# Top-32 attention and a gated feed-forward on one core: one operand of the pairwise minimum and maximum, and of the weights' bit operations, read from PSUM, under a planner with other durations

## The chip, the core and the metric

The kernel runs on one core of a Trainium2 chip. A core has TensorE (PE, matrix products), VectorE (DVE), ScalarE (ACT), GpSimd (POOL) and SyncE (SP, which here issues all DMAs). Each engine works through its own queue in order; a semaphore holds an instruction until what it needs is done. SBUF is the working memory, PSUM the eight banks that PE writes into. POOL does not read PSUM in this kernel. The metric is device microseconds of one execution; smaller is better.

## The reference, cut to what matters

```python
# q, k, v: (4 batches, 8 heads, 576, 64) float32
scores = scale * np.matmul(q, k.transpose(0, 1, 3, 2))
kth = np.partition(scores, -32, axis=-1)[..., -32:-31]
scores = np.where(scores >= kth, scores, -1e9)
attn = exp(scores - max); attn = attn / (sum + 1e-9)
x = matmul(attn, v)                       # heads side by side: (2304, 512)
xn = x / sqrt(mean(x * x) + 1e-6) * rms_g
g = xn @ w_gate                           # (2304, 1536)
out = (g * sigmoid(g) * (xn @ w_val)) @ w_out
```

The three weights arrive as float64 and are used as float32 in two parts, a rounded one and the remainder, so that products keep float32 accuracy.

## The kernel before, in words

**Plan.** `build` does not issue instructions; it adds operations to a `_Plan`, each with its engine, a duration, the tiles it reads and writes, at times a PSUM bank, and a priority `pri`. `emit` then runs a greedy list schedule (`place`): at each time every free engine takes the ready operation with the smallest key. Forward and backward passes alternate, each using the other's times as keys, and the order of the shortest plan found is what every engine's queue gets, DMA issues on SP included. The durations steer only this order; the hardware takes its own time. Banks fall into three groups: "a" (four banks: scores, transposes, value products, preparation of Q and K), "g" (two: gate and value products) and "o" (two: output products). A bank is chosen when the first operation on it is placed and is free after the last.

**Attention.** There are 72 steps; each handles two score tiles `e` of 128 queries by 576 keys. In `attend`, PE makes the scores of a tile in two halves of 288 columns, each in an "a" bank, and ScalarE copies each half into an SBUF tile `sp` (L523). `topk` then finds the 32nd largest of a row on VectorE: the pairwise minimum and maximum of the two halves (L497, L498), the 8 largest of the minima (L499), then four rounds of "8 largest" (L502) and three of "replace those 8" (L504). `bt` (L530) gathers the row's maximum and threshold times constants. ScalarE's Relu against the threshold (L534), GpSimd's subtraction (L535) and ScalarE's Exp (L536) make the masked weights; PE transposes them (L560), ScalarE copies (L562), and PE multiplies with V. The scores have four `sp` buffers, so PE may run ahead of VectorE.

The two lines that the change is about:

```python
add(DVE, 0.37, lambda: nc.vector.tensor_tensor(mn[:, e, :], a, b, op=ALU.min), r=spk, w=(nk,), pri=pri)
add(DVE, 0.37, lambda: nc.vector.tensor_tensor(row[:, 0:half], a, b, op=ALU.max), r=spk, w=(mk,), pri=pri)
```

**Feed-forward.** Each unit (256 tokens, early on 128) normalises its rows (small VectorE chains, L539 to L541 and L639 to L645; L628 scales rows out of a bank), transposes them, forms the two parts (ScalarE L658, VectorE L661), and makes gate and value products in "g" banks. Tanh, two products (L710 and L711, or GpSimd's L707 and L708 in place of L710), and a split into two parts (L722, L723) lead to the output products. All matmuls are recorded at L298, the helper that issues them.

**Weights.** During the first unit, `weight_piece` loads 36 pieces of 128 x 512 float64 as 32-bit words and rebuilds a float32 in a tile `t` with VectorE's bit operations: for the gate weights three instructions (L337 to L339), for the other two matrices two (L332, L333) with a correction by ScalarE and GpSimd (L334, L335). Each later one reads `t` as the one before wrote it. ScalarE and GpSimd then split `t` (L340, L343).

A second plan, `build(True)`, with thresholds from whole rows, is run only if a flag says that the shortcut of the pairs missed something; no instruction of it is in the profile.

Of the kernel before, what the change touches and what calls it, by code (L numbers as in the profile page):

```python
# [22 lines left out]
# Where an op's first key lies against its step's, and which forms some of the ops take.  # L23
# [14 lines left out]
class _Bank:  # L38
    """One PSUM bank's worth of data; the bank itself is chosen when the first op is placed."""
# [11 lines left out]
class _Plan:  # L51
    """Ops are added in an order in which they would be right one after another; emit() puts them
    out in the order of a greedy list schedule that keeps every dependency of that order."""
# [8 lines left out]
    def add(self, eng, dur, fn, r=(), w=(), bank=None, pri=0.0, nbytes=0):  # L62
        o = _Op()
        o.eng, o.dur, o.fn, o.pri, o.bank, o.nbytes = eng, dur, fn, pri, bank, nbytes
# [29 lines left out]
    def place(self, key, back=False):  # L94
        """A greedy list schedule, the op with the smallest key first; back: from the end. Returns its
        length and every op's start, or None if it gets stuck on the banks."""
# [5 lines left out]
        free = [0.0] * 4 + [0.0 if back else 0.45]  # L102
        avail = [0.0] * len(ops)
# [9 lines left out]
        while left:  # L113
            for e in range(5):
# [74 lines left out]
    def emit(self):  # L189
        """Schedules forwards and backwards by turns, each with the other's times as keys."""  # L190
# [19 lines left out]
def tile_topk_attention_moe(  # L210
# [80 lines left out]
    def build(exact):  # L291
        """The whole computation as a plan; exact: with the threshold from whole rows, and with the
        weights as they were left by the other one."""
# [20 lines left out]
        def weight_piece(src, half, hi, lo, keyh, keyl, pri):  # L314
            """[128, 512] of a weight as hi + lo. A float64 comes as its bits."""
# [8 lines left out]
            else:  # L324
# [4 lines left out]
                dma(raw, src.bitcast(U32), 524288, (), rk, pri - 2)  # L329
                if half:  # L330
                    ti, si = t.bitcast(I32), lo.bitcast(I32)
                    add(DVE, 0.336, lambda: nc.vector.tensor_scalar(tu, low, 29, None, op0=ALU.logical_shift_right), r=rk, w=tk, pri=pri)  # L332
                    add(DVE, 0.602, lambda: nc.vector.scalar_tensor_tensor(tu, top, 3, tu, op0=ALU.logical_shift_left, op1=ALU.bitwise_or), r=rk, w=tk, pri=pri)  # L333
                    add(ACT, 0.62, lambda: nc.scalar.activation(lo, top.bitcast(F32), AF.Sign), r=rk, w=(keyl,), pri=pri)  # L334
                    add(POOL, 1.23, lambda: nc.gpsimd.tensor_tensor(ti, ti, si, op=ALU.add), r=(keyl,), w=tk, pri=pri)  # L335
                else:
                    add(DVE, 0.336, lambda: nc.vector.tensor_scalar(tu, top, 3, 0x3FFFFFF8, op0=ALU.logical_shift_left, op1=ALU.bitwise_and), r=rk, w=tk, pri=pri)  # L337
                    add(DVE, 0.602, lambda: nc.vector.scalar_tensor_tensor(tu, top, 0xC0000000, tu, op0=ALU.bitwise_and, op1=ALU.bitwise_or), r=rk, w=tk, pri=pri)
                    add(DVE, 0.602, lambda: nc.vector.scalar_tensor_tensor(tu, low, 29, tu, op0=ALU.logical_shift_right, op1=ALU.bitwise_or), r=rk, w=tk, pri=pri)  # L339
            add(ACT, 0.52, lambda: nc.scalar.copy(hi, t), r=tk, w=(keyh,), pri=pri)  # L340
            add(
                POOL, 1.225,
# [4 lines left out]
        def weight_in(c, n, pri):  # L347
            """The nth of the 8 pieces of gate's and val's columns c * 512 and on."""
# [12 lines left out]
        ptc = [0, 0]  # L361

        def split(bank, hi, lo, keyh, keyl, pri):
# [5 lines left out]
            add(POOL, 1.225, lambda: nc.gpsimd.tensor_tensor(lo, tmp, hi.bitcast(F32), op=ALU.subtract), r=(keyh, tk), w=(keyl,), pri=pri)  # L369
# [64 lines left out]
        def prep_q_tile(b, tile, half, pri):  # L434
            """128 queries of four heads."""
# [35 lines left out]
        # A row of mx: the larger ones of the pairs (288), the 8 largest of the smaller ones, then the  # L471
        # rounds of eight, so that the last of those 8, the row's maximum and its 32nd are 15 apart.
# [5 lines left out]
        def topk(i, e, pri):  # L478
            """The 32 largest of a row: pairs' larger ones and the 8 largest of their smaller ones hold
            them unless a ninth smaller one is above the 32nd, which attend() notes down."""  # L480
# [15 lines left out]
            a, b = sp[s][:, e * S:e * S + half], sp[s][:, e * S + half:(e + 1) * S]  # L496
            add(DVE, 0.37, lambda: nc.vector.tensor_tensor(mn[:, e, :], a, b, op=ALU.min), r=spk, w=(nk,), pri=pri)  # L497
            add(DVE, 0.37, lambda: nc.vector.tensor_tensor(row[:, 0:half], a, b, op=ALU.max), r=spk, w=(mk,), pri=pri)  # L498
            add(DVE, 0.37, lambda: nc.vector.max(row[:, half:half + 8], mn[:, e, :]), r=(nk,), w=(mk,), pri=pri)  # L499
            for n in range(4):  # L500
                o8 = row[:, rounds[n]]
                add(DVE, 0.376, lambda o8=o8: nc.vector.max(o8, row[:, 0:half + 8]), w=(mk,), pri=pri + 0.1 * n)  # L502
                if n < 3:
                    add(DVE, 0.376, lambda o8=o8: nc.vector.match_replace(row[:, 0:half + 8], o8, row[:, 0:half + 8], NEG), w=(mk,), pri=pri + 0.1 * n)  # L504

        def attend(i, scores, qs, sums, pri):
            """scores(e): the (column in qh/ql, K slot) pairs that add up to tile e's scores."""
            s, t = i % NS, i % 2
            for e in range(2):
                for half in range(2):  # L510
# [11 lines left out]
                    add(PE, 0.252 * len(parts), sm, r=(("qh", qs), ("ql", qs)) + kk, w=(("sp", s, e, half),), bank=bank, pri=pri + PR["SO"])  # L522
                    add(ACT, 0.29, lambda bank=bank, c0=c0: nc.scalar.copy(sp[s][:, c0:c0 + 288], bank.tile[:, 0:288]), w=(("sp", s, e, half),), bank=bank, pri=pri + PR["SO"])  # L523
            for e in range(2):
                topk(i, e, pri + PR["TB"] * e)
# [3 lines left out]
            else:  # L529
                add(DVE, 0.075, lambda: nc.vector.tensor_tensor(bt[t], mx[:, :, 295:326:15], cst, op=ALU.mult), r=(("mx", 0, 0), ("mx", 1, 0)), w=(("bt", t),), pri=pri + PR["SM"])  # L530
                add(POOL, 0.154, lambda: nc.gpsimd.tensor_tensor(gap[:, i, :], bt[t][:, :, 0], bt[t][:, :, 2], op=ALU.subtract), r=(("bt", t),), w=(("gap", i),), pri=pri + PR["SM"])
            for e in range(2):
# [3 lines left out]
                add(ACT, 0.76, lambda e=e, tl=tl: nc.scalar.activation(tl, tl, AF.Exp, bias=bt[t][:, e, 1:2], scale=SCALE, accum_out=sums(e)[0]), r=(("bt", t),), w=spkeys(i, e) + (sums(e)[1],), pri=pri + PR["SM"])  # L536

        def invert(rslot, sl, keys, key, pri):
            add(DVE, 0.08, lambda: nc.vector.tensor_scalar(rs[rslot][sl], rs[rslot][sl], 1e-9, None, op0=ALU.add), w=keys, pri=pri)  # L539
            add(DVE, 0.09, lambda: nc.vector.reciprocal(ri[rslot][sl], rs[rslot][sl]), r=keys, w=(key,), pri=pri)  # L540
# [25 lines left out]
        def attend_out(i, j, pair, vs, pri):  # L566
# [9 lines left out]
            add(PE, 1.26, pv, r=(ck, ak, bk) + vkeys(vs), w=(("xv", j, pair),), bank=bank, pri=pri)  # L576
# [31 lines left out]
        wcount = [0, 0]  # L608

        def feed_forward(u, js, xs, xkeys, rslot, stores, pri, last=False):  # L610
            """For the tiles js of 128 tokens: both, or one."""
# [27 lines left out]
            add(DVE, 0.07, lambda: nc.vector.tensor_scalar(s_, s_, 1.0 / DM, 1e-6, op0=ALU.mult, op1=ALU.add), w=ssk, pri=fx)  # L639
            add(DVE, 0.07, lambda: nc.vector.tensor_scalar(w_.bitcast(I32), s_.bitcast(I32), 1, None, op0=ALU.logical_shift_right), r=ssk, w=rwk, pri=fx)  # L640
            add(DVE, 0.07, lambda: nc.vector.tensor_scalar(v_.bitcast(I32), w_.bitcast(I32), -1.0, float(0x5F3759DF), op0=ALU.mult, op1=ALU.add), r=rwk, w=rvk, pri=fx)
            for _ in range(3):
                add(DVE, 0.07, lambda: nc.vector.scalar_tensor_tensor(w_, v_, -0.5, v_, op0=ALU.mult, op1=ALU.mult), r=rvk, w=rwk, pri=fx)  # L643
                add(DVE, 0.07, lambda: nc.vector.tensor_tensor(w_, w_, s_, op=ALU.mult), r=ssk, w=rwk, pri=fx)
                add(DVE, 0.07, lambda: nc.vector.scalar_tensor_tensor(v_, w_, 1.5, v_, op0=ALU.add, op1=ALU.mult), r=rwk, w=rvk, pri=fx)  # L645
# [230 lines left out]
```

## Time and profile before

| | |
|---|---|
| median of 3 runs | 956.7 us (955.13 to 957.41) |
| span of the profiled execution | 955.8 us |
| mean granted TensorE clock | 0.946 |
| PE busy | 842.4 us (88%) |
| DVE busy | 834.2 us (87%) |
| ACT busy | 655.1 us (69%) |
| POOL busy | 540.2 us (57%) |

The profiled execution has no time of its own beside its span; the span lies between the three runs. A row of a stretch reads "from:to length, then for each engine busy us (instructions), the granted TensorE clock, the DMA share and GB/s"; for one source line it holds VectorE's busy time and count alone, then the same three. A row of one source line reads "engine, operation, out<-in, count: shortest/median/longest ns, first and last start". A row of a group reads "busy us, mean ns | idle time of the engine before it". A row of the timeline reads "start us, duration us, engine, line, operation". A row of waits reads "who <- for whom: us in total, times, longest". A recorded duration overlaps the next instruction's by about 0.08 us, so that differences of durations are used and not their sums.

### The profile page before, as it was taken

How to read it: one execution, taken by the hardware profiler on the slowest of the kernel's cores; microseconds unless marked ns; L12 is line 12 of the kernel's file. 1: busy time of each engine (PE TensorE's matmuls, PEld its weight loads, DVE VectorE, ACT ScalarE, POOL GpSimd, SP SyncE). 2: the span in 40 equal slices, each digit the busy share in tenths (PEclk: the TensorE clock that was granted, in tenths of full speed). 3: DMA queues.
4: the chain of work that ended last, by engine and by line, in shares of the span. 5: the costliest groups of instructions: out<-in, count | busy, mean ns of one | idle time of the engine just before them, and what ended most of it. 6: DMA issues, size and time to landing. Idle time of an engine off the chain costs nothing. (4 is left out here: it accounts for less than half of the span.)

```text
span 955.8 us, 19213 instructions
## 1 busy us (share of the span) xinstructions
PE 842.4 (88%) x6458; PEld 756.4 (79%) x6458; DVE 834.2 (87%) x2472; ACT 655.1 (69%) x1655; POOL 540.2 (57%) x564
## 2 busy tenths in 40 slices
PE   6655664778989999999999999998999999999996
PEld 4544554567778988998799889898999899899995
DVE  6999999999899999999889999999999929895221
ACT  6856565658878887887778788786877736765311
POOL 6756787696666754677656555565535423532111
PEclk9966786889999999999999999999999999999999
DMA  6432564345554333332443243343533433333433
GB/s 170 124 118 71 175 192 150 126 155 183 179 155 124 107 87 125 102 93 79 141 124 116 68 140 96 94 114 101 162 103 102 128 114 103 112 91 108 134 118 107
DMA packets 104573, 116.84 MB, mean 122 GB/s; under 512 B 68880, under 2 KB 82192, under 8 KB 104464
## 3 DMA queue, kind: packets, MB, share of 16 engines
q1 hardware_dynamic: 104464, 115.51, 39.7%
q8 instruction: 53, 0.87, 0.4%
q14 instruction: 56, 0.46, 0.2%
HBM read 104.47 MB, written 11.01 MB: 121 GB/s over the span
## 5 line engine op out<-in xcount | busy, mean ns | idle before, releaser
L502 DVE MAX8 mx<-mx 128x8 f32<-128x296 f32 x576 | 245.8, 453 | 0.9
L535 POOL TENSOR_TENSOR sp<-sp,rr 128x576 f32<-128x576 f32 x144 | 193.2, 1353 | 25.6 <-ACT rr L534 24.3
L504 DVE MATCH_REPLACE8 mx<-mx 128x296 f32<-128x296 f32 x432 | 191.9, 448 | 0.0
L723 POOL TENSOR_TENSOR hl<-tg,hh 128x256 fp32r<-128x256 f32 x108 | 82.9, 768 | 168.3 <-ACT hh L722 93.1
L298 PE MATMUL bank<-wo,hh 128*128 128x512 f32 x432 | 145.4, 418 | 1.4 <-DMA wo<-wosc 0.9
L534 ACT ACTIVATE rr<-sp,bt 128x576 bf16<-128x576 f32 x144 | 109.1, 778 | 49.2 <-DVE bt L530 49.0
L298 PE MATMUL bank<-kt,qh 128*128 128x288 f32 x320 | 109.1, 353 | 25.3 <-ACT sp L523 6.5
L560 PE MATMUL bank<-ident,sp 128*128 128x128 f32 x648 | 103.6, 290 | 28.7 <-ACT sp L536 16.9
L536 ACT ACTIVATE sp<-sp,bt 128x576 f32<-128x576 f32 x144 | 113.2, 786 | 17.3 <-POOL sp L535 16.3
L298 PE MATMUL bank<-xth,wgh 128*128 128x256 f32 x384 | 112.5, 293 | 0.0
L560 PEld LDWEIGHTS bank<-ident,sp 128*128 128x128 f32 x648 | 79.0, 148 | 42.1 <-ACT sp L536 20.3
L523 ACT COPY sp<-bank 128x288 f32<-128x288 f32 x288 | 105.3, 408 | 8.5 <-PE bank L298 8.2
L298 PE MATMUL bank<-xth,wvh 128*128 128x256 f32 x384 | 110.3, 287 | 0.0
L298 PE MATMUL bank<-xtl,wgh 128*128 128x256 f32 x384 | 107.5, 280 | 0.0
L298 PE MATMUL bank<-xth,wgl 128*128 128x256 f32 x384 | 107.5, 280 | 0.0
L298 PE MATMUL bank<-xtl,wvh 128*128 128x256 f32 x384 | 107.5, 280 | 0.0
L298 PE MATMUL bank<-xth,wvl 128*128 128x256 f32 x384 | 107.5, 280 | 0.0
L298 PE MATMUL bank<-kt,ql 128*128 128x288 f32 x320 | 98.4, 318 | 9.8 <-POOL ql L369 9.8
L298 PEld LDWEIGHTS bank<-kt,qh 128*128 128x128 f32 x320 | 66.2, 207 | 40.4 <-ACT sp L523 10.5
L497 DVE TENSOR_TENSOR mn<-sp 128x288 f32<-128x288 f32 x144 | 88.2, 613 | 11.4 <-ACT sp L523 11.1
L562 ACT COPY pt<-bank 128x512 f32<-128x512 f32 x144 | 84.5, 594 | 17.4 <-PE bank L560 16.7
L710 DVE SCALAR_TENSOR_TENSOR tg<-tg,bank 128x256 f32<-128x256 f32 x76 | 31.2, 411 | 73.1 <-ACT tg L704 72.7
(161 smaller groups left out, 2255.1 us busy)
## 6 DMA issues: line engine op xcount, KB each, us to landing
wo<-wosc SPq DMA_DIRECT2D x108, 512.0 KB, 3.3
vt<-in_v_dram SPq DMA_DIRECT2D x52, 256.0 KB, 3.2
qraw<-in_q_dram SPq DMA_DIRECT2D x112, 64.0 KB, 2.8
xvt<-in_moe_w_gate_dram SPq DMA_DIRECT2D x12, 512.0 KB, 3.7
wosc<-wo SPq DMA_DIRECT2D x12, 512.0 KB, 3.9
kraw<-in_k_dram SPq DMA_DIRECT2D x32, 128.0 KB, 3.0
kraw<-in_moe_w_val_dram SPq DMA_DIRECT2D x8, 512.0 KB, 4.0
out_dram<-osb SPq DMA_DIRECT2D x14, 256.0 KB, 2.9
```

The lines of the kernel that those rows point to most:

```text
L298: nc.tensor.matmul(o, l, r, start=start, stop=stop)
L497: add(DVE, 0.37, lambda: nc.vector.tensor_tensor(mn[:, e, :], a, b, op=ALU.min), r=spk, w=(nk,), pri=pri)
L502: add(DVE, 0.376, lambda o8=o8: nc.vector.max(o8, row[:, 0:half + 8]), w=(mk,), pri=pri + 0.1 * n)
L504: add(DVE, 0.376, lambda o8=o8: nc.vector.match_replace(row[:, 0:half + 8], o8, row[:, 0:half + 8], NEG), w=(mk,), pri=pri + 0.1 * n)
L523: add(ACT, 0.29, lambda bank=bank, c0=c0: nc.scalar.copy(sp[s][:, c0:c0 + 288], bank.tile[:, 0:288]), w=(("sp", s, e, half),), bank=bank, ...
L534: add(ACT, 0.67, lambda e=e, tl=tl: nc.scalar.activation(rr[e], tl, AF.Relu, bias=bt[t][:, e, 2:3], scale=-BIG), r=(("bt", t),) + spkeys(i ...
L535: add(POOL, 1.24, lambda e=e, tl=tl: nc.gpsimd.tensor_tensor(tl, tl, rr[e], op=ALU.subtract), r=(("rr", e),), w=spkeys(i, e), pri=pri + PR ...
L536: add(ACT, 0.76, lambda e=e, tl=tl: nc.scalar.activation(tl, tl, AF.Exp, bias=bt[t][:, e, 1:2], scale=SCALE, accum_out=sums(e)[0]), r=(("b ...
L560: nc.tensor.transpose(bank.tile[:, c * 128:(c + 1) * 128], sp[s][:, c0 + c * 128:c0 + (c + 1) * 128], ident)
L562: add(ACT, 0.05 + n * 128 / 1200, lambda dst=dst, bank=bank, n=n: nc.scalar.copy(dst[:, 0:n * 128], bank.tile[:, 0:n * 128]), w=(key,), ba ...
L710: add(DVE, 0.335, lambda gb=gb, hs=hs: nc.vector.scalar_tensor_tensor(th[hs], th[hs], 1.0, gb.tile[:, 0:256], op0=ALU.add, op1=ALU.mult), ...
L723: add(POOL, 0.69, lambda hs=hs: nc.gpsimd.tensor_tensor(hl[hs], th[hs], hh[hs].bitcast(F32), op=ALU.subtract), r=(("th", hs), ("hh", hs)), ...
```

## The change

The first half's score bank goes to `topk`, and minimum and maximum take their first operand from it; the second half comes from `sp` as before. Halves are made in the order 1, 0, so that the bank held longer is filled last. It is free after the maximum. In `weight_piece` the intermediate words go to an "a" bank in place of `t`; only the last VectorE instruction writes `t`. The one-operand shift thereby writes PSUM instead of SBUF.

The planner gets a flag `sh` for the remaining VectorE instructions that compete with GpSimd (`bt`, the sum's addition in `invert`, the small chains of the normalisation): in forward passes such an instruction and a GpSimd instruction are not placed at the same time. Many durations are changed; the priorities `PR` and the latencies are not. In the second plan the halves come in the same new order, and `topk` does not use the bank.

```diff
-    def add(self, eng, dur, fn, r=(), w=(), bank=None, pri=0.0, nbytes=0):
+    def add(self, eng, dur, fn, r=(), w=(), bank=None, pri=0.0, nbytes=0, sh=False):
...
+        port = {DVE: 0.0, POOL: 0.0}
...
+                if e == POOL and not back and port[DVE] > t + 1e-9:
+                    continue
                 while ready[e]:
                     item = heapq.heappop(ready[e])
+                    if ops[item[1]].sh and not back and port[POOL] > t + 1e-9:
+                        held.append(item)
+                        continue
...
+                if e == POOL or o.sh:
+                    port[e] = end
...
+            for x in () if back else port.values():
+                if t + 1e-9 < x < nxt:
+                    nxt = x
...
+                bank = _Bank("a")
                 if half:
-                    add(DVE, 0.336, lambda: nc.vector.tensor_scalar(tu, low, 29, None, op0=ALU.logical_shift_right), r=rk, w=tk, pri=pri)
-                    add(DVE, 0.602, lambda: nc.vector.scalar_tensor_tensor(tu, top, 3, tu, op0=ALU.logical_shift_left, op1=ALU.bitwise_or), r=rk, w=tk, pri=pri)
+                    add(DVE, 0.6, lambda: nc.vector.tensor_scalar(bank.tile.bitcast(U32), low, 29, None, op0=ALU.logical_shift_right), r=rk, bank=bank, pri=pri)
+                    add(DVE, 0.6, lambda: nc.vector.scalar_tensor_tensor(tu, top, 3, bank.tile.bitcast(U32), op0=ALU.logical_shift_left, op1=ALU.bitwise_or), r=rk, w=tk, bank=bank, pri=pri)
...
-                    add(DVE, 0.602, lambda: nc.vector.scalar_tensor_tensor(tu, top, 0xC0000000, tu, op0=ALU.bitwise_and, op1=ALU.bitwise_or), r=rk, w=tk, pri=pri)
-                    add(DVE, 0.602, lambda: nc.vector.scalar_tensor_tensor(tu, low, 29, tu, op0=ALU.logical_shift_right, op1=ALU.bitwise_or), r=rk, w=tk, pri=pri)
...
+                    add(DVE, 0.6, lambda: nc.vector.scalar_tensor_tensor(bank.tile.bitcast(U32), top, 0xC0000000, bank.tile.bitcast(U32), op0=ALU.bitwise_and, op1=ALU.bitwise_or), r=rk, bank=bank, pri=pri)
+                    add(DVE, 0.6, lambda: nc.vector.scalar_tensor_tensor(tu, low, 29, bank.tile.bitcast(U32), op0=ALU.logical_shift_right, op1=ALU.bitwise_or), r=rk, w=tk, bank=bank, pri=pri)
...
-        def topk(i, e, pri):
+        def topk(i, e, bank, pri):
...
-            a, b = sp[s][:, e * S:e * S + half], sp[s][:, e * S + half:(e + 1) * S]
-            add(DVE, 0.37, lambda: nc.vector.tensor_tensor(mn[:, e, :], a, b, op=ALU.min), r=spk, w=(nk,), pri=pri)
-            add(DVE, 0.37, lambda: nc.vector.tensor_tensor(row[:, 0:half], a, b, op=ALU.max), r=spk, w=(mk,), pri=pri)
+            b, bk = sp[s][:, e * S + half:(e + 1) * S], (("sp", s, e, 1),)
+            add(DVE, 0.365, lambda: nc.vector.tensor_tensor(mn[:, e, :], bank.tile[:, 0:half], b, op=ALU.min), r=bk, w=(nk,), bank=bank, pri=pri)
+            add(DVE, 0.365, lambda: nc.vector.tensor_tensor(row[:, 0:half], bank.tile[:, 0:half], b, op=ALU.max), r=bk, w=(mk,), bank=bank, pri=pri)
...
-                    add(DVE, 0.376, lambda o8=o8: nc.vector.match_replace(row[:, 0:half + 8], o8, row[:, 0:half + 8], NEG), w=(mk,), pri=pri + 0.1 * n)
+                    add(DVE, 0.434, lambda o8=o8: nc.vector.match_replace(row[:, 0:half + 8], o8, row[:, 0:half + 8], NEG), w=(mk,), pri=pri + 0.1 * n)
...
+            firsts = []
             for e in range(2):
-                for half in range(2):
+                for half in (1, 0):
...
-                    add(PE, 0.252 * len(parts), sm, r=(("qh", qs), ("ql", qs)) + kk, w=(("sp", s, e, half),), bank=bank, pri=pri + PR["SO"])
+                    add(PE, 0.266 * len(parts), sm, r=(("qh", qs), ("ql", qs)) + kk, w=(("sp", s, e, half),), bank=bank, pri=pri + PR["SO"])
...
+                    if half == 0:
+                        firsts.append(bank)
             for e in range(2):
-                topk(i, e, pri + PR["TB"] * e)
+                topk(i, e, firsts[e], pri + PR["TB"] * e)
```

Among the other durations: the gate and value products 0.654 to 0.7, the output products 0.648 to 0.7, the value products of attention 1.26 to 1.3, GpSimd's `gap` 0.154 to 0.2, ScalarE's parts of the normalised rows 0.16 to 0.25, VectorE's 0.2 to 0.257; the rest move by a few per cent.

More of the change, by code (lines that the diff above doesn't have):

```diff
@@ new lines, in weight_piece @@
+                    add(DVE, 0.6, lambda: nc.vector.scalar_tensor_tensor(tu, top, 3, bank.tile.bitcast(U32), op0=ALU.logical_shift_left, op1=ALU.bitwise_or), r=rk, w=tk, bank=bank, pri=pri)
+                    add(ACT, 0.57, lambda: nc.scalar.activation(lo, top.bitcast(F32), AF.Sign), r=rk, w=(keyl,), pri=pri)
+                    add(POOL, 1.24, lambda: nc.gpsimd.tensor_tensor(ti, ti, si, op=ALU.add), r=(keyl,), w=tk, pri=pri)
+                else:
+                    add(DVE, 0.6, lambda: nc.vector.tensor_scalar(bank.tile.bitcast(U32), top, 3, 0x3FFFFFF8, op0=ALU.logical_shift_left, op1=ALU.bitwise_and), r=rk, bank=bank, pri=pri)
+                    add(DVE, 0.6, lambda: nc.vector.scalar_tensor_tensor(bank.tile.bitcast(U32), top, 0xC0000000, bank.tile.bitcast(U32), op0=ALU.bitwise_and, op1=ALU.bitwise_or), r=rk, bank=bank, pri=pri)
+                    add(DVE, 0.6, lambda: nc.vector.scalar_tensor_tensor(tu, low, 29, bank.tile.bitcast(U32), op0=ALU.logical_shift_right, op1=ALU.bitwise_or), r=rk, w=tk, bank=bank, pri=pri)
@@ L340, in weight_piece @@
             add(ACT, 0.52, lambda: nc.scalar.copy(hi, t), r=tk, w=(keyh,), pri=pri)
             add(
-                POOL, 1.225,
+                POOL, 1.24,
                 lambda: nc.gpsimd.tensor_tensor(lo, t, hi.bitcast(F32), op=ALU.subtract),
@@ L521, in attend @@
                     kk = tuple(("kt", ks, z) for _, ks in parts for z in (e, 2))
-                    add(PE, 0.252 * len(parts), sm, r=(("qh", qs), ("ql", qs)) + kk, w=(("sp", s, e, half),), bank=bank, pri=pri + PR["SO"])
-                    add(ACT, 0.29, lambda bank=bank, c0=c0: nc.scalar.copy(sp[s][:, c0:c0 + 288], bank.tile[:, 0:288]), w=(("sp", s, e, half),), bank=bank, pri=pri + PR["SO"])
+                    add(PE, 0.266 * len(parts), sm, r=(("qh", qs), ("ql", qs)) + kk, w=(("sp", s, e, half),), bank=bank, pri=pri + PR["SO"])
+                    add(ACT, 0.285, lambda bank=bank, c0=c0: nc.scalar.copy(sp[s][:, c0:c0 + 288], bank.tile[:, 0:288]), w=(("sp", s, e, half),), bank=bank, pri=pri + PR["SO"])
+                    if half == 0:
+                        firsts.append(bank)
             for e in range(2):
-                topk(i, e, pri + PR["TB"] * e)
+                topk(i, e, firsts[e], pri + PR["TB"] * e)
             if exact:
@@ L529, in attend @@
             else:
-                add(DVE, 0.075, lambda: nc.vector.tensor_tensor(bt[t], mx[:, :, 295:326:15], cst, op=ALU.mult), r=(("mx", 0, 0), ("mx", 1, 0)), w=(("bt", t),), pri=pri + PR["SM"])
-                add(POOL, 0.154, lambda: nc.gpsimd.tensor_tensor(gap[:, i, :], bt[t][:, :, 0], bt[t][:, :, 2], op=ALU.subtract), r=(("bt", t),), w=(("gap", i),), pri=pri + PR["SM"])
+                add(DVE, 0.075, lambda: nc.vector.tensor_tensor(bt[t], mx[:, :, 295:326:15], cst, op=ALU.mult), r=(("mx", 0, 0), ("mx", 1, 0)), w=(("bt", t),), pri=pri + PR["SM"], sh=True)
+                add(POOL, 0.2, lambda: nc.gpsimd.tensor_tensor(gap[:, i, :], bt[t][:, :, 0], bt[t][:, :, 2], op=ALU.subtract), r=(("bt", t),), w=(("gap", i),), pri=pri + PR["SM"])
             for e in range(2):
@@ L575, in pv @@
                         mm(bank.tile[64 * e:64 * e + 64, 0:128], vv[:, e * 256 + c * 64:e * 256 + (c + 1) * 64], src[:, c * 128:(c + 1) * 128], False, c == 3)
-            add(PE, 1.26, pv, r=(ck, ak, bk) + vkeys(vs), w=(("xv", j, pair),), bank=bank, pri=pri)
+            add(PE, 1.3, pv, r=(ck, ak, bk) + vkeys(vs), w=(("xv", j, pair),), bank=bank, pri=pri)
             add(ACT, 0.16, lambda: nc.scalar.copy(xv[:, pair, j * 128:(j + 1) * 128], bank.tile[:, 0:128]), w=(("xv", j, pair),), bank=bank, pri=pri + PR["EV"])
@@ L657, in feed_forward @@
                     dh, dl = xth[:, c, j * 128:(j + 1) * 128], xtl[:, c, j * 128:(j + 1) * 128]
-                    add(ACT, 0.16, lambda bank=bank, cs=cs, g=g, dh=dh: nc.scalar.mul(dh, bank.tile[:, cs], g), r=("gt",), w=(("xth", c, j),), bank=bank, pri=fx)
+                    add(ACT, 0.25, lambda bank=bank, cs=cs, g=g, dh=dh: nc.scalar.mul(dh, bank.tile[:, cs], g), r=("gt",), w=(("xth", c, j),), bank=bank, pri=fx)
                     add(
-                        DVE, 0.2,
+                        DVE, 0.257,
                         lambda bank=bank, cs=cs, g=g, dh=dh, dl=dl: nc.vector.scalar_tensor_tensor(dl, bank.tile[:, cs], g, dh.bitcast(F32), op0=ALU.mult, op1=ALU.subtract),
```

33 lines of the change are left out of this document (15 added, 18 removed).

## The prediction

> **What bounds the kernel now.** I read the page first, then the busy time by stretches, then the duration spread of single lines, and last the timeline around one slow instruction. The page gives the span, the shares, and the 40 slices:
>
> ```profile
> span 955.8 us, 19213 instructions
> PE 842.4 (88%) x6458; PEld 756.4 (79%) x6458; DVE 834.2 (87%) x2472; ACT 655.1 (69%) x1655; POOL 540.2 (57%) x564
> ...
> PE   6655664778989999999999999998999999999996
> ...
> DVE  6999999999899999999889999999999929895221
> ...
> PEclk9966786889999999999999999999999999999999
> ```
>
> PE and DVE look equally loaded, but not at the same time. The stretches, cut where the picture changes, show it:
>
> ```profile
> core 0: us, PE busy (x) PEld busy (x) DVE busy (x) ACT busy (x) POOL busy (x), PEclk, DMA share, GB/s
> 0.00:40.00 40.00, 27.73 (x128) 21.23 (x128) 32.31 (x89) 31.21 (x78) 26.04 (x37) 1.00 0.54 143
> 40.00:220.00 180.00, 111.02 (x667) 94.28 (x666) 179.92 (x414) 108.59 (x251) 132.87 (x109) 0.77 0.44 138
> 220.00:300.00 80.00, 72.22 (x588) 63.72 (x587) 75.29 (x238) 65.90 (x176) 54.00 (x62) 0.96 0.58 180
> 300.00:750.00 450.00, 434.74 (x3590) 397.10 (x3589) 432.78 (x1372) 350.71 (x901) 268.68 (x289) 0.99 0.37 108
> 750.00:956.00 206.00, 196.69 (x1494) 180.09 (x1492) 113.92 (x363) 98.67 (x253) 58.66 (x68) 0.99 0.36 113
> ```
>
> From 40 to 220 us DVE is never idle (179.92 of 180), while PE does 111 us of work at a granted clock of 0.77. From 300 us on PE is the limit: 434.74 + 196.69 of 656 us leave it 24.6 us idle. So **a microsecond taken from DVE before 220 us moves everything behind it forward; one taken after 300 us is worth a small part of itself.**
>
> Now the durations of single lines (min/median/max in ns): the two pairwise lines with both operands in SBUF, then three lines that read one operand from a PSUM bank.
>
> ```profile
> L497 DVE TENSOR_TENSOR mn<-sp x144: 401/449/2239, 10.8 to 855.4; 128x288 f32<-128x288 f32 x144
> L498 DVE TENSOR_TENSOR mx<-sp x144: 439/450/1556, 11.2 to 858.3; 128x288 f32<-128x288 f32 x144
> L711 DVE TENSOR_TENSOR tg<-tg,bank x108: 371/408/422, 104.4 to 945.7; 128x256 f32<-128x256 f32 x108
> L661 DVE SCALAR_TENSOR_TENSOR xtl<-bank,gt,xth x72: 323/340/352, 84.3 to 896.6; 128x128 fp32r<-128x128 f32 x72
> L628 DVE TENSOR_TENSOR x<-bank,ri x16: 666/678/693, 71.1 to 878.1; 128x512 f32<-128x512 f32 x16
> ```
>
> The SBUF pair has a tail up to 2239 ns over a median of 449; the 196 instructions with a PSUM operand have none at all (their largest is 14, 12 and 15 ns above the median) although POOL works beside them too. What the tail is shows in the timeline (start us, duration us):
>
> ```profile
> 299.74 1.33 POOL L369 TENSOR_TENSOR ql<-pt,qh 128x512 fp32r<-128x512 f32 x1
> 300.23 1.16 DVE L497 TENSOR_TENSOR mn<-sp 128x288 f32<-128x288 f32 x1
> ```
>
> POOL's instruction ends at 301.07, and the pairwise minimum, begun in its middle, ends 0.32 us later at 301.39. It stood still until POOL was through. I read this as DVE and POOL excluding each other when a DVE instruction streams two SBUF operands.
>
> **The change, part by part.** *Pairwise minimum and maximum.* The stretches of L497 (three rows) and of L498 (three rows):
>
> ```profile
> 40.00:220.00 180.00, 18.40 (x22) 0.77 0.44 138
> 220.00:300.00 80.00, 10.39 (x15) 0.96 0.58 180
> 300.00:750.00 450.00, 48.50 (x85) 0.99 0.37 108
> ...
> 40.00:220.00 180.00, 17.25 (x22) 0.77 0.44 138
> 220.00:300.00 80.00, 7.76 (x14) 0.96 0.58 180
> 300.00:750.00 450.00, 49.44 (x86) 0.99 0.37 108
> ```
>
> No row shows 288 elements from PSUM. L711 (256 elements, 408 ns) and L628 (512, 678 ns) lie around it; the straight line between them gives 408 + 270 x 32/256 = 442 ns. I take 0.45 us, the undisturbed SBUF median. Saved from 40 to 220: 18.40 + 17.25 - 44 x 0.45 = 15.9 us; from 220 to 300: 18.15 - 29 x 0.45 = 5.1; from 300 to 750: 97.94 - 171 x 0.45 = 21.0. Bounds for the first: at L711's 0.408 it is 17.7; if the exclusion stays it is 0.
>
> [...]
>
> *Weights' bit operations.* From 40 to 220 us, lines 332, 333 (val and out weights), 337, 338, 339 (gate weights), in this order, and three undisturbed instructions of them:
>
> ```profile
> 40.00:220.00 180.00, 16.88 (x22) 0.77 0.44 138
> 40.00:220.00 180.00, 21.48 (x23) 0.77 0.44 138
> 40.00:220.00 180.00, 9.04 (x10) 0.77 0.44 138
> 40.00:220.00 180.00, 8.87 (x10) 0.77 0.44 138
> 40.00:220.00 180.00, 11.86 (x10) 0.77 0.44 138
> ...
> L332 DVE TENSOR_SCALAR qrt<-tg x1: 401/401/401, 52.7 to 52.7; 128x512 uint32<-128x512 uint32 x1
> L333 DVE SCALAR_TENSOR_TENSOR x<-tg,x x1: 677/677/677, 39.7 to 39.7; 128x512 uint32<-128x512 uint32 x1
> L338 DVE SCALAR_TENSOR_TENSOR qrt<-xvt,qrt x5: 677/680/1487, 20.5 to 166.0; 128x512 uint32<-128x512 uint32 x5
> ```
>
> That is 68.1 us for 75 instructions. The two-operand forms should fall to 0.68 us. The one-operand shift (32 of the 75) now writes PSUM, which no row shows: between 0.40 us (it stays as quick as from SBUF to SBUF) and 0.69 us (L628's slowest, 512 elements with PSUM). I take 0.68, as L628 is the nearest row that touches PSUM with 512 elements. Then 75 x 0.68 = 51.0 and 17.1 us are saved. Bounds: 17.1 + 32 x 0.28 = 26.1 saved if the shift stays quick; 32 x 0.28 = 9.0 lost if the exclusion stays and the shift gets slower.
>
> *How much of 33.0 us (15.9 + 17.1) is exposed.* DVE covers the whole stretch, so all of it is, until another engine takes over. POOL is next: 132.87 us of work in 180 would be 90% of 147. POOL gets some time back too, as it is also held:
>
> ```profile
> L535 POOL TENSOR_TENSOR sp<-sp,rr 128x576 f32<-128x576 f32 x21 | 30.7, 1469 | 1.0 <-ACT rr L534 1.0
> ...
> L535 POOL TENSOR_TENSOR sp<-sp,rr x144: 1275/1294/1736, 26.0 to 868.3; 128x576 f32<-128x576 f32 x144
> ```
>
> From 40 to 220 us this line's mean is 1469 ns against a median of 1294 over the whole trace, 21 x 0.175 = 3.7 us. At nearly 90% load waits between POOL, ACT and DVE are sure to appear, so I take three quarters of 33.0: 25 us. Of the 5.1 us from 220 to 300 (DVE 75.29 of 80) I take half, 2.5. Of the 21.0 after 300 only what fills PE's gaps counts: 15.3 us idle from 300 to 750, of which a fifth, 3.
>
> *The held bank.* A first half's score bank used to be free after ScalarE's copy (L523); now it waits for DVE's minimum and maximum. Two of the four "a" banks are held per step, and behind them queue PE's next scores, the transposes (L560) and the value products, all in PE's order. Today's lead of the scores over the minimum, in the step near 306 us, and what PE waits for on these copies:
>
> ```profile
> 305.70 1.88 ACT L523 COPY sp<-bank 128x288 f32<-128x288 f32 x6
> 308.80 0.45 DVE L497 TENSOR_TENSOR mn<-sp 128x288 f32<-128x288 f32 x1
> PEld bank L298 <- ACT sp L523: 12.0, 17, 2.1
> ```
>
> The hold is about 3.1 us of a step that takes (300 to 750: 85 minima, two to a step, in 450 us) 10.6 us. PE's other work, the feed-forward products in banks of the "g" and "o" groups, covers it; without that cover it is 3.1 us a step. I take a loss of 2 us in all, between 0 and the rival below. The weights' banks are held only from one DVE instruction to the next.
>
> *The planner.* New durations, POOL and DVE shut out against each other, halves in the order 1, 0: this moves every instruction in every queue, SP's DMA issues included. The stretches leave 24.6 us of PE idle after 300 us to gain and far more to lose; I take 0.
>
> Sum: -25 - 2.5 - 3 + 2 = **-28.5 us**. The profiled span, 955.8 us, lies inside the three runs (955.13 to 957.41), 0.9 below their median; the sum is on the span, 927.3, and on the median **928**.
>
> **The rivals.** *More* (chance 0.12): the planner also keeps the remaining two-operand instructions out of POOL's way.
>
> ```profile
> L530 DVE TENSOR_TENSOR bt<-mx,cst 128x6 f32<-128x6 f32 x72 | 22.6, 314 | 0.7
> L644 DVE TENSOR_TENSOR rw<-rw,ss 128x2 f32<-128x2 f32 x24 | 8.7, 361 | 0.3
> L530 DVE TENSOR_TENSOR bt<-mx,cst x72: 147/157/1277, 23.8 to 865.9; 128x6 f32<-128x6 f32 x72
> ```
>
> L530 loses 22.6 - 72 x 0.157 = 11.3 us to it over the whole run, about a sixth of the steps before 220 us. With the whole 33 us exposed, 5 from 220 to 300, 2 of L530's in the front and 6 of PE's gaps: 956.7 - 46 = 911. Against: every instruction that the planner holds back for POOL delays the softmax behind it.
>
> *Less* (0.12): POOL and the chain L530, Relu, subtraction, Exp set the front once DVE is lighter. Then the front shortens only by what POOL itself gets back, some 10 us (3.7 of L535 and as much again of the weights' subtractions, with a little idle): 956.7 - 10 - 2.5 - 1 = 943. For: POOL's 90%. Against: 47 us of POOL idle in this stretch.
>
> *Slower* (0.12): the held banks stall PE after 220 us, where PE is the limit. The rows of L497 from 220 to 750 us hold 15 + 85 minima, 50 steps. The stall eats the gain from 28.5/50 = 0.57 us a step; at 0.8 us, about a quarter of the 3.1 us hold, it is 928 + 40 = 968. For: "a" serves scores, transposes and value products alike, and PE has no slack. Against: two banks stay free, and the planner counts the banks.
>
> *It does not do what it says* (0.03): PSUM operands are held by POOL as well; nothing is saved, the shift loses 9.0 us: 966. Against: 196 instructions without a tail. *No change* (0.04): the planner's new order costs what DVE gains, 957.
>
> **How the numbers follow.** The forecast, 928 (918 to 940 from three quarters to all of the front exposed and a few us of the planner's order), has 0.57. Runs of this kernel can tell about 0.2%, 2 us, from no change. Faster: 0.57 + 0.12 + 0.12 = 0.81; same 0.04; slower 0.12 + 0.03 = 0.15. The range takes in the forecast, *more* and *less*: 906 to 953, which leaves 0.19 out.
>
> **What would show it.** Right: the new pairwise lines have no tail, maximum under 0.6 us; the shift takes 0.6 to 0.7 us; DVE's busy total falls by some 44 us for the pairs (15.9 + 5.1 + 21.0 and a little outside) plus some 17 for the weights; PE's stretch at 9 tenths begins some 25 us earlier, and the time from there to the end stays near 656 us. Wrong: a tail on the new pairwise lines; DVE idle between 40 and 190 us with POOL at 9 tenths (*less*); PE waiting for DVE's maximum, in a row that does not exist today, by more than 28 us (*slower*); or PE's idle time spread over new causes after 220 us, which would put it on the planner's order.

## The result, and the profile after

The changed kernel takes 928.5 us (median of 4 runs, 926.2 to 929.6) against 957.1 us beside it: ratio 0.9704, 95% interval 0.9686 to 0.9723, 28.6 us faster. 928 was forecast. The total came out as worked out; where the microseconds came from did not.

The page of the changed kernel:

```profile
span 927.7 us, 19332 instructions
PE 839.8 (91%) x6458; PEld 747.8 (81%) x6458; DVE 759.1 (82%) x2472; ACT 658.8 (71%) x1655; POOL 494.6 (53%) x564
...
PE   5775976589889998999999999999999999999996
...
DVE  6999899894979999999879999989799937884221
...
PEclk9955987897989999999999999999999999999999
```

DVE's busy time fell by 75 us (834.2 to 759.1) and POOL's by 46 (540.2 to 494.6), with the same instructions. PE's hardly moved. The time fell by 28.

The duration spreads of the new pairwise lines and of the weights' operations (shortest/median/longest ns):

```profile
L510 DVE TENSOR_TENSOR mn<-bank,sp x144: 408/451/479, 11.0 to 830.6; 128x288 f32<-128x288 f32 x144
...
L511 DVE TENSOR_TENSOR mx<-bank,sp x144: 406/448/482, 11.3 to 831.4; 128x288 f32<-128x288 f32 x144
...
L345 DVE TENSOR_SCALAR bank<-kraw x14: 671/691/702, 40.0 to 202.8; 128x512 uint32<-128x512 uint32 x14
...
L346 DVE SCALAR_TENSOR_TENSOR x<-kraw,bank x5: 687/689/689, 85.8 to 194.2; 128x512 uint32<-128x512 uint32 x5
```

The tails are gone to the last instruction (482 ns at most for the pairs, 2239 before; 711 ns at most for the weights), an instruction of the pair costs 0.45 us, and the one-operand shift costs 0.69 us, near the 0.68 that was assumed. Before, that shift had a tail too, though it has only one SBUF operand:

```profile
L332 DVE TENSOR_SCALAR qrt<-kraw x5: 408/416/1493, 92.5 to 212.4; 128x512 uint32<-128x512 uint32 x5
```

To see **where** the time went, the two kernels are cut at the same work. First the thresholds `bt` (L530 before, L546 after), one for each of the 72 steps, and GpSimd's split of the gated rows (L723 before, L739 after), 108 in all. Before, to 310 us and from there to 700 us, first L530, then L723:

```profile
0.00:310.00 310.00, 9.09 (x22) 0.86 0.48 148
310.00:700.00 390.00, 9.04 (x36) 0.99 0.37 108
...
0.00:310.00 310.00, 12.23 (x15) 0.86 0.48 148
310.00:700.00 390.00, 37.08 (x48) 0.99 0.37 108
```

After, to 296 us and from there to 673 us, first L546, then L739:

```profile
0.00:296.00 296.00, 4.26 (x22) 0.84 0.51 153
296.00:673.00 377.00, 9.25 (x36) 1.00 0.39 115
...
0.00:296.00 296.00, 10.99 (x15) 0.84 0.51 153
296.00:673.00 377.00, 35.35 (x48) 1.00 0.39 115
```

The counts agree exactly: 22 steps and 15 splits take 310 us before and 296 after; the next 36 and 48 take 390 and 377. So **at these cuts the front gave 14 us, the middle 13, the end about 1**, each good to some 3 us (at 293 us the changed kernel has 21 steps, at 302 it has 16 splits). The two plans order their work differently, so a cut elsewhere gives another share; one at 220 us stands further below. The engines' busy time in the same three stretches, before:

```profile
0.00:310.00 310.00, 220.96 (x1460) 188.42 (x1461) 297.52 (x771) 213.39 (x524) 219.32 (x214) 0.86 0.48 148
310.00:700.00 390.00, 375.10 (x3103) 342.04 (x3102) 373.11 (x1179) 307.03 (x793) 236.54 (x258) 0.99 0.37 108
700.00:956.00 256.00, 246.34 (x1899) 225.96 (x1897) 163.59 (x524) 134.66 (x341) 84.38 (x93) 0.99 0.36 112
```

and after:

```profile
0.00:296.00 296.00, 223.44 (x1430) 182.08 (x1431) 254.28 (x774) 215.97 (x521) 195.23 (x213) 0.84 0.51 153
296.00:673.00 377.00, 369.56 (x3129) 339.85 (x3128) 342.72 (x1167) 305.05 (x787) 218.01 (x257) 1.00 0.39 115
673.00:928.00 255.00, 246.83 (x1903) 225.89 (x1901) 162.07 (x533) 137.82 (x350) 81.40 (x95) 0.99 0.35 111
```

In the front DVE has 43.2 us less to do (297.5 to 254.3) and the stretch is 14 us shorter; in the middle it is 30.4 (373.1 to 342.7) and 13. About a third and two fifths came through, in the part that was forecast at three quarters and in the part that was forecast at a seventh. The rest became DVE idle time: 12.5 to 41.7 us in the front, 16.9 to 34.3 in the middle. What DVE waits for in the first 310 us of the changed kernel (us in total, times, longest) is spread over many causes:

```profile
DVE bank L350 <- DMA xvt<-in_moe_w_gate_dram: 9.3, 2, 7.6
DVE tg L727 <- POOL tg L724: 6.5, 1, 6.5
DVE mn L510 <- ACT sp L537: 6.4, 7, 1.6
DVE rs L555 <- ACT sp L552: 5.5, 2, 4.6
DVE xtl L677 <- ACT xth L674: 3.0, 1, 3.0
```

### The profile page after: what moved, and what is told of

It is laid out like the page before. It is cut to its first block, busy times and chain, and to the rows that moved or that the text cites. A ratio compares the mean times of both kernels' runs of the same rounds, so it can differ in the third digit from the quotient of the medians.

```text
span 927.7 us, 19332 instructions
## 1 busy us (share of the span) xinstructions
PE 839.8 (91%) x6458; PEld 747.8 (81%) x6458; DVE 759.1 (82%) x2472; ACT 658.8 (71%) x1655; POOL 494.6 (53%) x564
## 4 chain that ended last, share of the span: by engine, by line
PE 70%; DVE 14%; ACT 6%; DMA 2%; issue 2%; POOL 1%; POOLq 0%; DVEq 0%; ACTq 0%; SPq 0%
PE bank L309 59%; PE bank L576 6%; DVE mx L515 3%; DVE mx L517 3%; PE bank L404 1%; DVE bank L345 1%; ACT pt L578 1%; ACT sp L537 1%; PE bank L442 1%; DVE mx L512 1%; DVE mx L511 1%; PE bank L636 1%; DMA kraw<-in_k_dram 1%; DVE mn L510 1%; DVE xtl L677 1%
## 5 line engine op out<-in xcount | busy, mean ns | idle before, releaser
L515 DVE MAX8 mx<-mx 128x8 f32<-128x296 f32 x576 | 248.5, 461 | 1.7
L551 POOL TENSOR_TENSOR sp<-sp,rr 128x576 f32<-128x576 f32 x144 | 183.6, 1289 | 44.3 <-ACT rr L550 43.3
L517 DVE MATCH_REPLACE8 mx<-mx 128x296 f32<-128x296 f32 x432 | 194.0, 455 | 0.0
L739 POOL TENSOR_TENSOR hl<-tg,hh 128x256 fp32r<-128x256 f32 x108 | 79.5, 736 | 172.2 <-ACT hh L738 92.8
L576 PE MATMUL bank<-ident,sp 128*128 128x128 f32 x648 | 107.7, 292 | 27.4 <-ACT sp L552 8.0
L309 PE MATMUL bank<-kt,qh 128*128 128x288 f32 x320 | 107.1, 347 | 20.3 <-ACT pt L578 6.8
L578 ACT COPY pt<-bank 128x512 f32<-128x512 f32 x144 | 84.4, 594 | 23.1 <-PE bank L576 19.7
L309 PE MATMUL bank<-kt,ql 128*128 128x288 f32 x320 | 95.2, 310 | 0.0
L309 PEld LDWEIGHTS bank<-kt,qh 128*128 128x128 f32 x320 | 64.2, 201 | 35.7 <-ACT pt L578 10.5
L720 ACT ACTIVATE tg<-bank 128x256 f32<-128x256 f32 x108 | 41.4, 383 | 71.9 <-PE bank L309 71.2
```

The costliest lines, as they stand in the source:

```text
L309: nc.tensor.matmul(o, l, r, start=start, stop=stop)
L517: add(DVE, 0.434, lambda o8=o8: nc.vector.match_replace(row[:, 0:half + 8], o8, row[:, 0:half + 8], NEG), w=(mk,), pri=pri + 0.1 * n)
L551: add(POOL, 1.24, lambda e=e, tl=tl: nc.gpsimd.tensor_tensor(tl, tl, rr[e], op=ALU.subtract), r=(("rr", e),), w=spkeys(i, e), pri=pri + PR ...
L576: nc.tensor.transpose(bank.tile[:, c * 128:(c + 1) * 128], sp[s][:, c0 + c * 128:c0 + (c + 1) * 128], ident)
L578: add(ACT, 0.05 + n * 128 / 1200, lambda dst=dst, bank=bank, n=n: nc.scalar.copy(dst[:, 0:n * 128], bank.tile[:, 0:n * 128]), w=(key,), ba ...
L720: add(ACT, 0.27, lambda gb=gb, hs=hs: nc.scalar.activation(th[hs], gb.tile[:, 0:256], AF.Tanh, scale=1.0 if halves[0] else 0.5), w=(("th", ...
```

## The experiments

Each time is the median of its runs; each ratio is to the kernel before on the same chip. Differences to the changed kernel are differences of these ratios times 957 us.

### Is it the exclusion? The pairs from SBUF, order kept

```diff
+            a = sp[s][:, e * S:e * S + half]
-            ... nc.vector.tensor_tensor(mn[:, e, :], bank.tile[:, 0:half], b, op=ALU.min) ...
+            ... nc.vector.tensor_tensor(mn[:, e, :], a, b, op=ALU.min) ...
```

(the maximum likewise)

> The changed kernel with its order of every queue kept, except that minimum and maximum read their first operand from the SBUF copy again (the bank is still held in the plan until the maximum). Only the exclusion against POOL comes back. Theory A (the gain is the exclusion, and DVE's time counts in the middle too): the pairs get their tail back, DVE's busy time rises by some 40 us and the time by 15 to 27 us, to 943 to 955, more than half of it after 300 us. Theory B (as predicted: all from the front, after 300 us DVE's time is worth a seventh): 940 to 945, with no more than 4 us of the rise after 300 us. Theory C (the planner's order brings the gain): at most 933.

Measured: 977.4 us, ratio 1.021 (1.0182 to 1.0238), 48 us slower than the changed kernel and 20 slower than before. The groups of the pairs (busy us, mean ns):

```profile
L511 DVE TENSOR_TENSOR mn<-sp 128x288 f32<-128x288 f32 x144 | 96.2, 676 | 28.0 <-ACT sp L538 24.9 <-POOL tg L724 2.7
L512 DVE TENSOR_TENSOR mx<-sp 128x288 f32<-128x288 f32 x144 | 89.9, 643 | 0.0
```

The tails are back, (96.2 + 89.9) - (64.0 + 62.1 in the changed kernel) = 60 us. No instruction changed its place in any queue, so the operand's memory alone makes this difference: theory C falls. (The minimum now also needs ScalarE's copy of the first half, but what VectorE waits for ScalarE before it is no more: 24.9 us against 27.1 in the changed kernel.) Theory A's mechanism holds, but its bound was too low: the time rose by four fifths of the 60 us. GpSimd loses time with the pairs in SBUF as well: where they are put back under a new plan (the pairs undone, below), its busy total is 521.0 us, 26 more than in the changed kernel. One minimum of this run shows the exclusion at its plainest; POOL, then DVE (start us, duration us):

```profile
13.79 1.26 POOL L356 TENSOR_TENSOR wgl<-x,wgh 128x512 fp32r<-128x512 f32 x1
15.02 0.72 POOL L400 TENSOR_TENSOR kraw<-kraw 128x256 fp32r<-128x256 f32 x1
15.70 1.28 POOL L382 TENSOR_TENSOR ql<-pt,qh 128x512 fp32r<-128x512 f32 x1
16.94 1.27 POOL L356 TENSOR_TENSOR wvl<-osb,wvh 128x512 fp32r<-128x512 f32 x1
18.18 0.72 POOL L400 TENSOR_TENSOR kraw<-kraw 128x256 fp32r<-128x256 f32 x1
...
14.18 5.03 DVE L511 TENSOR_TENSOR mn<-sp 128x288 f32<-128x288 f32 x1
```

The minimum lasts 5.03 us: it starts while POOL is at work, and five POOL instructions follow each other without a gap. It ends 0.31 us after the fifth (18.90).

### The planner alone

```diff
+                if e == POOL and not back and port[DVE] > t + 1e-9:
+                    continue
...
-            add(DVE, 0.37, ... op=ALU.min), r=spk, w=(nk,), pri=pri)
+            add(DVE, 0.365, ... op=ALU.min), r=spk, w=(nk,), pri=pri, sh=True)
```

> The kernel before with the changed planner alone: the new durations, the exclusion rule, and the pairs and the weights' bit operations marked as excluding POOL (the one-operand shift keeps its 0.336 us); all operands stay in SBUF. Theories A and B: DVE's time for pairs and bit operations still has to be paid, as a tail or as an order around POOL: 948 to 960. Theory C: 928 to 938.

Measured: 967.2 us, ratio 1.0113 (1.0095 to 1.0131): slower than before by 11 us, outside every theory's range. The groups of maximum and minimum:

```profile
L509 DVE TENSOR_TENSOR mx<-sp 128x288 f32<-128x288 f32 x144 | 82.4, 582 | 0.0
L508 DVE TENSOR_TENSOR mn<-sp 128x288 f32<-128x288 f32 x144 | 78.7, 547 | 10.5 <-ACT sp L534 10.2
```

Planned apart from POOL, the pairs still meet it: 582 and 547 ns against 611 and 613 before. Each queue keeps its order, but not the plan's clock. That small drifts make them meet again, and that the plan pays for keeping them apart, is argued, not shown. This plan also marks the pairs and the bit operations, which the changed kernel does not.

### The operands alone

```diff
-... sh=True)
+... )                                  (nothing is marked, so the rule never applies)
-                    add(DVE, 0.434, ... match_replace ...
+                    add(DVE, 0.376, ... match_replace ...      (and all durations of before)
```

> The changed kernel with the operands in PSUM and the banks held, but planned with the durations of before and without the exclusion rule. Theories A and B: 926 to 938, the tails of pairs and bit operations are gone whatever the order. Theory C: 948 or more.

Measured: 938.5 us, ratio 0.981 (0.979 to 0.983), 10 us behind the changed kernel; half a microsecond above what A and B expected. Operands alone bring 18 of the 28 us, and the planner alone brings a loss: the remaining 10 us were seen only on top of the new operands.

### The rule or the durations

```diff
-                if e == POOL and not back and port[DVE] > t + 1e-9:
-                    continue
...
-... pri=pri + PR["SM"], sh=True)
+... pri=pri + PR["SM"])
```

> The changed kernel with its operands and its new durations, but without the rule that keeps VectorE's marked instructions and GpSimd apart in the plan. With old durations and no rule it was 938. If the durations make the difference to 928: 924 to 932. If the rule makes it: 935 to 941.

Measured: 926.5 us, ratio 0.9684 (0.9666 to 0.9702), 2 us under the changed kernel, with intervals that overlap. The rule brings nothing that can be measured; the durations make the 10 us. Among them, the replacements were planned 0.058 us short each, 432 x 0.058 = 25 us of DVE time, and the 36 shifts into PSUM at 0.336 us in place of 0.6, 36 x 0.264 = 9.5 us; which of the durations make the difference is not shown. The row of engines says something more:

```profile
PE 842.1 (91%) x6458; PEld 749.3 (81%) x6458; DVE 781.4 (84%) x2472; ACT 658.4 (71%) x1655; POOL 493.5 (53%) x564
```

Without the rule VectorE is busy 22 us more than in the changed kernel (`bt` takes 18.7 us in all against 15.9; where the rest lies is not shown), and the time is no longer. So 22 of the 75 us that DVE's busy time fell by went with the rule, and they brought no time.

### More DVE time: middle, front, and with the plan told

```diff
+            def least(again=1 if 20 <= i < 60 else 0):     # front: 3 if 2 <= i < 16
+                for _ in range(1 + again):
+                    nc.vector.tensor_tensor(mn[:, e, :], bank.tile[:, 0:half], b, op=ALU.min)
-            add(DVE, 0.365, lambda: ... op=ALU.min), ...
+            add(DVE, 0.365, least, ...                     # told: 0.73 for these steps
```

> The changed kernel, order kept, with each pairwise minimum of steps 20 to 59 (about 285 to 695 us) issued twice: 80 instructions more at 0.365 us from start to start, 29 us of DVE time where PE looks full. Theory B (PE is the limit there, a seventh counts): 931 to 934. Theory A (DVE's time counts there): 943 to 957.

Measured: 959.3 us, ratio 1.0035 (1.0018 to 1.0051): 29 us more DVE time cost 32 us, more than even theory A allowed. Theory B's seventh falls at once. VectorE's busy time rose by 40 us, not by 29 (798.8 against 759.1): among the rest, `bt` took 23.1 us in all against 15.9.

> The changed kernel, order kept, with each pairwise minimum of steps 2 to 15 issued four times: 84 instructions more at 0.365 us, 31 us of DVE time, in the front. If the front is paced by DVE: 950 to 960. If DVE's idle time of the front takes it in: 932 to 945.

Measured: 965.4 us, ratio 1.0091 (1.0066 to 1.0116): 31 us cost 37 us, above both ranges, although DVE stands idle 41.7 us in the front of the changed kernel. Here too the busy time rose by more, 38 us (797.4 against 759.1). The TensorE clock granted to three of these four executions was 0.92 (0.95 in the changed kernel), but the one at 0.944 took 965.2 us as well, so the clock does not explain it.

> The same doubled minima of steps 20 to 59 as in the run before this set (29 us of DVE time), but with 0.73 us in the plan, so that every queue's order takes them into account. If the full price in the fixed order came from the order (PE waiting in its queue for a late DVE): 928 to 940. If DVE sets the pace of the middle: 948 to 960.

Measured: 940.6 us, ratio 0.9827 (0.9795 to 0.9859): the same 29 us cost 12 us when the order is made for them, just above the first range. So most of the full price in the middle is the order, not a lack of DVE time; for the front this was not tried.

### Less DVE time, and less PE time

```diff
+                    def replace(o8=o8, left=20 <= i < 60 and n in (2,)):     # front: 2 <= i < 16 and n in (1, 2)
+                        if not left:
+                            nc.vector.match_replace(...)
```

> The changed kernel, order kept, without the last of the three replacements (L517) in steps 20 to 59: the top 24 are kept there in place of the top 32. 80 x 0.434 = 35 us of DVE time less, between about 285 and 695 us. More DVE time there cost its full length; if DVE sets the pace there (A), less of it gives back at least half, 893 to 911. If a late DVE only holds up PE's fixed queue, and PE is the limit as predicted (B), a seventh at most comes back: 922 to 929.

Measured: 928.05 us, ratio 0.971 (0.9689 to 0.9731). The row of engines:

```profile
PE 838.9 (91%) x6458; PEld 747.3 (81%) x6458; DVE 731.2 (79%) x2312; ACT 658.4 (71%) x1655; POOL 494.5 (53%) x564
```

DVE's busy time is 28 us less than in the changed kernel (35 by the durations of the plan, 80 x 0.434) and the time is the same. About as much DVE work as cost 32 us when added gives nothing when taken away.

> The changed kernel, order kept, without the last two replacements in steps 2 to 15 (the top 16 are kept there): 28 x 2 x 0.434 = 24 us of DVE time less, between about 30 and 230 us. Front still paced by DVE, as predicted: three quarters or more come back, 904 to 911. Front now held by other engines and by the order (DVE stood idle 42 us in the first 310 of the changed kernel, against 12 before): 916 to 929.

Measured: 927.1 us, ratio 0.9683 (0.9657 to 0.971): 24 us less DVE time in the front (20 by the busy total, 739.2) give 2 us, which the intervals don't tell from none. It is the second reading, not the one predicted.

```diff
-                                for n, (wt, xt) in enumerate(((wh, xth), (wh, xtl), (wl, xth))):
+                                for n, (wt, xt) in enumerate(((wh, xth), (wl, xth), (wh, xtl))):
+                                    if n == 1 and 3 <= u < 7:
+                                        continue
```

> The changed kernel, order of the queues kept, without the product of the weights' low part with the rows' high part in the feed-forward units 3 to 6 (gate and value, about 365 to 727 us): 384 of the 256-column matmuls fewer, about 45 us of PE's time at 0.117 us from one to the next. There, 35 us of DVE time less gave nothing back. If PE sets the pace of the middle (as predicted): 884 to 900. If PE's busy share there is mostly waiting, and the fixed order of all queues sets the pace: 915 to 929.

Measured: 920.0 us, ratio 0.9604 (0.9584 to 0.9624). Its row of engines, and its stretch from 296 to 673 us:

```profile
PE 810.6 (88%) x6074; PEld 704.1 (77%) x6074; DVE 758.6 (82%) x2472; ACT 655.9 (71%) x1655; POOL 494.7 (54%) x564
...
296.00:673.00 377.00, 351.56 (x2851) 309.88 (x2849) 347.79 (x1185) 307.31 (x802) 220.41 (x259) 1.00 0.39 115
```

About 45 us of PE's time less (384 matmuls at 0.117 us each; the weight loads are busy 44 us less) give 10 us, the second reading. Most of them lie in the stretch in which PE was busy 369.56 of 377 us, so PE's work alone did not set the time there.

### The parts undone, planned anew

```diff
-            ... bank.tile[:, 0:half], b, op=ALU.min), r=bk, w=(nk,), bank=bank, pri=pri)
+            ... a, b, op=ALU.min), r=spk, w=(nk,), pri=pri)
```

> The changed kernel without the pairs' part: minimum and maximum read SBUF, no bank is held, planned anew (they are not marked as excluding POOL, their durations stay 0.365 us); the weights' bit operations stay in PSUM. With the operands in SBUF the fixed order gave 977. If the held bank cost nothing and the tails are the whole price: 950 to 970. If holding the bank costs much of what the pairs gain: 930 to 940.

Measured: 967.6 us, ratio 1.0121 (1.0097 to 1.0146). Without the pairs' part the kernel is 40 us slower than the changed one, so what holding the bank costs is small beside what the tails cost; how much it is, this run does not say. Nothing here marks the pairs, the weights are in PSUM, and yet it is as slow as the planner alone (967.2): the marks are not needed for the loss, and why a new plan loses with the pairs in SBUF stays open.

```diff
-                bank = _Bank("a")
-                    add(DVE, 0.6, ... tensor_scalar(bank.tile.bitcast(U32), low, 29, ...
+                    add(DVE, 0.336, ... tensor_scalar(tu, low, 29, ...          (and so on, as before)
```

> The changed kernel without the weights' part: bit operations in SBUF in place, no bank for them, planned anew (0.336 and 0.6 us, not marked as excluding POOL); the pairs stay in PSUM. The prediction's 17 us of DVE time at three quarters: 938 to 945. If the weights' part brings nothing, as the front's small gain suggests: 924 to 932.

Measured: 938.35 us, ratio 0.9804 (0.9787 to 0.982): the weights' part is worth 10 us of the 28. This is the lower edge of the range that follows from the prediction's 17 us. The two parts sum to 50 us, while the kernel with the planner alone is 39 us behind the changed one (1.0113 against 0.9704): the parts do not add up. That each, undone alone, leaves a plan that fits the other worse is a reading, not shown.

## Why the prediction was right, and where its steps failed

**The mechanism was right.** The pairs with two SBUF operands wait for POOL (2239 and 1556 ns at the longest before), with one in PSUM they do not (479 and 482). The tail-free rows after the change, and the 48 us that return when the operand goes back with the order kept, show it. The prediction drew it a little too narrow: the one-operand shift from SBUF to SBUF waits too (416 ns in the middle, 1494 at most; one of 1493, begun at 212.40 us, ends 0.28 us after POOL's L335), while the 8 largest (L502) and the replacements (L504), also from SBUF to SBUF, never last more than 473 and 459 ns before. The rival that the change does not do what it says fell.

**The prices of the instructions were right**: 0.45 us for a pair (assumed 0.45), 0.69 for the shift (assumed 0.68). An operand in PSUM does not make the pair slower here: 451 and 448 ns in the middle, against 449 and 450 from SBUF before. DVE's busy time for all the work to 310 us fell by 43 us, where 33.0 + 5.1 = 38 were worked out for pairs and weights from 40 to 300.

**The step that failed first is that a microsecond taken before 220 us "moves everything behind it forward".** Up to there three quarters, 25 us, is about what came. The changed kernel's rows:

```profile
0.00:40.00 40.00, 26.38 (x98) 19.28 (x98) 30.80 (x94) 30.55 (x74) 21.94 (x37) 1.00 0.50 138
40.00:193.00 153.00, 106.57 (x655) 83.22 (x655) 142.91 (x413) 108.94 (x254) 107.30 (x100) 0.77 0.49 150
193.00:220.00 27.00, 22.25 (x153) 19.59 (x152) 20.36 (x65) 19.99 (x46) 23.42 (x26) 0.81 0.65 202
```

At 193 us it has done 507 instructions on VectorE and 328 on ScalarE; the kernel before had done 503 and 329 at 220 us, by the prediction's rows. PE (753 of 795) and GpSimd (137 of 146) get there some 7 and 9 us later, by their rates in the third row. So it is about 18 to 27 us ahead there, counted in instructions, which is a rough measure. At 310 us of the kernel before it is 14 us ahead. From 220 to 310 us, where 2.5 us more were to be gained, some 4 to 13 were lost, and VectorE came to stand idle (6.6 of 27 us in the third row; never from 40 to 220 before). What lost them is not shown; one sign is that the last shift of the weights, which the feed-forward needs, starts only 10 us earlier (202.8 against 212.4). The reason given for the discount, POOL at 90%, was wrong: POOL's own busy time shrank with the tails (540.2 to 494.6 us over the run), and it is busy 107 of 153 us (70%) from 40 to 193. After the change the front is not held by DVE alone: taking 24 us more from DVE there gives no more than 2.

**The step that failed second is "from 300 us on PE is the limit".** The middle was to give 3 us; it gave 13. The 24.6 us of PE idle time came from a row that counts a matmul as busy for its whole recorded length, and these overlap: in the changed kernel's timeline (start us, duration us)

```profile
401.63 0.28 PE L309 MATMUL bank<-xtl,wgh 128*128 128x256 f32 x1
401.75 0.28 PE L309 MATMUL bank<-xth,wgl 128*128 128x256 f32 x1
401.86 0.28 PE L309 MATMUL bank<-xth,wgh 128*128 128x256 f32 x1
```

a matmul is recorded at 0.28 us and the next starts 0.12 us later, so a wait of up to 0.16 us between them leaves no gap. The run with less PE work shows that PE had more room than that row says: 45 us less of its work moved the end by 10. The weight loads were busy 340 of 377 us there (90%), which would hardly have warned either.

So **the forecast of 928 was right by luck, through two errors that cancel**: 13.5 us too much for the front up to 310 us (27.5 against 14), and 10 us too little for the middle (3 against 13).

**What stands in their place** is an asymmetry that the runs show for the order of the changed kernel: DVE time put in behind the plan's back cost its whole length, in the middle (29 us: +32) and in the front (31 us: +37); DVE time taken away without a new plan gave nothing (35 us: 0; 24 us: -2); and time that the plan knew of cost less than half (29 us: +12, in the middle). That the kernel before paid for its tails as lateness of this kind is the likeliest reading, but it is not shown by itself, and not all unforeseen time costs: without the rule VectorE is busy 22 us more, and the time is no longer. Why only 28 of DVE's 75 us came back is not settled beyond those 22: the order of before was itself made with too short durations, and how much of the tails its own waits took in was not measured.

**The held bank.** 2 us were taken. PE's waits for the maximum, which exist only after the change:

```profile
PE bank L669 <- DVE mx L511: 4.5, 1, 4.5
...
PE bank L576 <- DVE mx L511: 2.1, 2, 1.8
...
PE bank L309 <- DVE mx L511: 1.0, 1, 1.0
```

These are 7.6 us in four waits, nearer the 2 than the 28 that *slower* needed. Their effect on the end was not tried by itself.

**The planner** was put at 0. With the operands in SBUF it costs 11 us (the planner alone, with more marks), with them in PSUM its durations are worth 10 (the operands alone, against the changed kernel and the one without the rule). Near 0 was wrong on either side; that *more* depended on the exclusion rule is refuted by the run without the rule. L530's tail did fall, from 22.6 us in all to 15.9, and brought nothing that the time shows: the run without the rule, where it is 18.7, takes no longer.

## What to carry to other kernels

Where every queue has a fixed order that a plan wrote, removing an instruction's unforeseen delay and telling the plan the true durations are best done as one piece of work: here the operands alone gave 18 us, the plan alone lost 11, both gave 28. To price an edit, don't read the busiest engine and its idle time in a stretch; cut both kernels at equal work, at more than one place, and compare; and test with a small added and a small removed load on the same instruction, since the two answers can differ from full price to nothing. Two VectorE operands in SBUF beside a busy GpSimd are worth looking for in any trace: a median of 449 ns with a tail to 2239 was their mark here, and an operand that lay in PSUM anyway removed it (482 at most).

## What the hardware showed that was not expected

- A VectorE instruction that waited for GpSimd was not served between two GpSimd instructions that followed each other closely: one minimum of the run with the pairs from SBUF stood through five of them, 5.03 us in place of 0.45.
- GpSimd loses time to the exclusion as well: its busy total fell from 540.2 to 494.6 us with the same 564 instructions, and 26 us come back in the run with the pairs undone, planned anew (521.0). Of the 46, the small subtraction `gap` gives 17 (31.1 to 14.0) and L535 10 (193.2 to 183.6), the line from which the prediction read 3.7 for its stretch.
- A VectorE instruction with one operand in PSUM and one in SBUF costs at 288 float32 elements what two in SBUF cost undisturbed (451 and 449 ns), while a one-operand shift of 512 words goes from 0.40 us (SBUF to SBUF) to 0.69 (into PSUM).
